# The convolution kernel's spectrum with its time signal as the stationary operand and ACT moving the result, and the first eight powers of each channel made in the setup

## The chip, the core and the metric

The kernel runs on one core of a Trainium2 chip. The metric is the device time of one execution in microseconds. A core has TensorE (PE, matrix products into PSUM; PEld are its weight loads), VectorE (DVE), ScalarE (ACT), GpSimd (POOL) and SyncE (SP, which here issues nearly all DMAs). Each has its own in-order instruction queue and they wait for each other by semaphores.

## What is computed

Two pairs of layers on 2048 tokens of 512 channels, all float32: a long convolution (an S4D layer) and then a feed-forward layer for the two tokens with the highest router score. Both pairs use the same weights. The part that matters here is the convolution and its kernel `K`:

```python
dt = jnp.exp(log_dt)
A = -jnp.exp(log_A_real) + 1j * A_imag
C = (C_real + 1j * C_imag) * dt[:, None]
P = jnp.exp((A * dt[:, None])[:, :, None] * pos[None, None, :])   # 512 channels, 128 states, 2048 positions
K = 2.0 * jnp.einsum("dn,dnl->dl", C, P).real
Kf = jnp.fft.rfft(K, L2)
Uf = jnp.fft.rfft(u_t, L2)
y = jnp.fft.irfft(Uf * Kf[None, :, :], L2)[:, :, :L]
return y + u * D_skip[None, None, :]

x = x + _A_ref(_layernorm(x), ...)
x = x + _B_ref(_layernorm(x), ...)     # two routed tokens
x = x + _A_ref(_layernorm(x), ...)
x = x + _B_ref(_layernorm(x), ...)
```

`K` doesn't depend on the tokens. The kernel makes its spectrum once, uses it in the first convolution as it comes and keeps it in DRAM (`kfd`) for the second.

## The kernel before

**Chunks and steps.** The 512 channels are four chunks of 128. The kernel's spectrum is made in 32 steps of sixteen channels (`KStep`, L434; eight steps a chunk). A position is written as `64 a + b`, with 32 values of `a` (coarse) and 64 of `b` (fine): with 128 states on the partitions, a step makes coarse and fine powers of sixteen channels (32 rows of 32 powers) and contracts them over the states to 32 x 64 values a channel.

**Setup** (`setup`, L324) computes for each channel and state a phase and a decay, and from them planes: plane 0 the start, planes 1 to 6 the steps of 1, 2, 4, ... powers (phases as shifted integers, decays as repeated products), as coarse and fine pairs. Chunk 0's planes go straight into `pi` and `pf` in SBUF (`direct`). Those of chunks 1 to 3 are made beside the first steps, in room that other tiles need later, stored in DRAM (`pid`, `prd`, one DMA for each plane, `put`, L345) and loaded half a chunk at a time (`load_params`, L294).

**One step u** has these parts:
- `phase_init` and `decay_init` (ACT, L446, L456) copy the starts into `ph` and `mg`; `phase` and `decay` (POOL, L452, L461) double what is there five times each, from 1 to 2, 4, 8, 16 and 32 powers, each time by one plane; a sixth `decay` makes `ml`.
- `trig` (ACT, L469): sine, absolute value and cosine of the 32 (and one) phases, into `sc`.
- `products` (DVE and POOL, L478): the decays into the sines and cosines. `ON_POOL` (L137) says which of them POOL takes.
- `contract` (PE, L491): 32 products of 128 rows into `pk`, four of 32 columns beside each other; ACT copies `pk` into `kt`.
- `spectrum` (L501): DVE adds the skip weight `D_skip` at position 0 of `kt`; then eight PE products with the constant `d1k` as the stationary operand (64 columns) and `kt` as the moving one (128 columns, 64 apart) into `kq`.
- `turn` (DVE, L514): a transpose in 32 by 32 blocks from `kq` into `gk`, the chunk's whole first stage.

`pk` and `kq` have one buffer each; `ph`, `mg`, `ml`, `sc` and `kt` two.

**Pipeline.** `slot(t)` (L720) issues step t-1's `spectrum`, step t's `products`, step t+1's `trig`, `phase_init` of t+3, `decay_init` of t+2, `phase` of t+2 and `decay` of t+1 in turns, then the `turn` of t-1 and the `contract` of t, with the convolution's own work between these at the places that `CONV1` (L32) gives: normalization (ACT), first stage `zf` (PE, and a DVE transpose), `kx` (the spectrum's second stage from `gk`, PE) and its way over `kfd` in DRAM back to SBUF, products with the spectrum (DVE, L568), `pv` (PE, L579), copies (ACT, L580), last stage (DVE, PE), statistics (DVE). The first six slots and the late setup are ordered by a scheduler, with `OPENING` (L112) as the order of issue; from slot 6 on DVE, ACT and POOL keep the written order (`in_order`, L211), while PE's order comes from the scheduler. When the 32 steps are done their tiles are given up, and the weights of the routed layer are loaded in their place; the rest (chunk 3's end, routed layer, second convolution, routed layer) holds no step of `KStep`.

## Time and profile before

| what | value |
| --- | --- |
| time, median of 3 runs | 697.32 us (696.2 to 698.96) |
| profiled execution, span from first to last instruction | 695.2 us |
| PE busy | 485.8 us, 70% |
| DVE busy | 580.9 us, 84% |
| ACT busy | 311.1 us, 45% |
| POOL busy | 500.4 us, 72% |
| data moved by DMA | 97.64 MB |

The profile is of one execution; its own time is its span and what lies around it, of which the page shows only the span. The runs' median is 2.1 us above that span. The page gives the span in 40 slices of 17.4 us, groups of like instructions (count, busy time, mean of one, the idle time of the engine just before them and what ended it) and DMA issues. Further views used below are busy times by stretches, the timeline of one engine, and the chain of waits that ended last.

### The profile page before, as it was taken

To read this page: it belongs to the slowest core of one execution; us is meant where nothing else is said; L and a number is where in the kernel's file an instruction comes from. 1 tells how busy PE (TensorE), PEld (TensorE's weight loads), DVE (VectorE), ACT (ScalarE), POOL (GpSimd) and SP (SyncE) were. 2 spreads that over 40 slices of the span, in tenths; PEclk is the share of its full clock that TensorE was granted. 3 is DMA by queue.
4 is the path that set the end of the run, shared out by engine and by line. 5 is a ranking of instruction groups with operands and counts; after the bars stand their busy time and mean duration, and the time that the engine had idled before them with its cause. 6 is when DMAs were issued, how large, how long until landed. Compare 5 with 4: busy or idle time off the path is not lost.

```text
span 695.2 us, 14060 instructions
## 1 busy us (share of the span) xinstructions
PE 485.8 (70%) x5300; PEld 360.2 (52%) x5300; DVE 580.9 (84%) x1164; ACT 311.1 (45%) x587; POOL 500.4 (72%) x659
## 2 busy tenths in 40 slices
PE   1012433798988898979789987267799888888336
PEld 1001322577855786648776665034678565656112
DVE  7899998687899999989999964985356799999950
ACT  4445645456753647527473121321511615214272
POOL 4879999999999999987993083260257766757252
PEclk9999775699998989979999998769599899999858
DMA  7961204768410977109460699600813748438436
GB/s 212 225 150 72 90 30 144 262 195 234 118 33 28 218 214 171 53 16 245 117 172 2 184 307 345 164 2 11 178 55 86 154 103 176 145 98 239 108 79 180
DMA packets 51709, 97.64 MB, mean 140 GB/s; under 512 B 4885, under 2 KB 35513, under 8 KB 47161
## 3 DMA queue, kind: packets, MB, share of 16 engines
q1 hardware_dynamic: 51512, 96.72, 51.5%
q8 instruction: 42, 0.69, 0.4%
q14 instruction: 27, 0.21, 0.1%
q0 software_dynamic: 128, 0.02, 0.0%
HBM read 70.23 MB, written 26.48 MB: 139 GB/s over the span
## 4 chain that ended last, share of the span: by engine, by line
DVE 33%; POOL 21%; DMA 16%; PE 14%; issue 8%; SPq 6%; ACT 1%; POOLq 0%; DVEq 0%; ACTq 0%
POOL mg L465 6%; DVE vt L638 6%; POOL ph L454 6%; PE zf L593 4%; DVE g L597 3%; DMA x<-in_x 3%; DVE jn L654 3%; DMA xw<-xs 3%; DVE p L609 3%; SPq L561 3%; DMA kf<-kfd 3%; DMA x<-xs 3%; POOL sc L482 2%; POOL ml L467 2%; DVE p L568 2%
## 5 line engine op out<-in xcount | busy, mean ns | idle before, releaser
L465 POOL TENSOR_TENSOR mg<-mg,pf 128x128 f32<-128x128 f32 (+4 forms) x160 | 108.6, 682 | 5.4 <-ACT pf L423 3.1
L454 POOL TENSOR_TENSOR ph<-ph,pi 128x512 int32<-128x512 int32 (+4 forms) x160 | 112.0, 702 | 0.5
L497 PE MATMUL pk<-sc 128*32 128x64 f32 x2048 | 46.3, 247 | 74.2 <-DVE sc L489 63.5
L618 POOL TENSOR_TENSOR y<-p 64x256 f32<-64x256 f32 x76 | 55.9, 736 | 50.0 <-DVE p L609 35.6
L507 PE MATMUL kq<-kt,d1k 128*64 128x128 f32 x512 | 63.4, 402 | 30.8 <-DVE kt L503 22.5
L593 PE MATMUL zf<-z,d 128*128 128x256 f32 x256 | 80.1, 453 | 5.9 <-DVE g L597 5.1
L497 PEld LDWEIGHTS pk<-sc 128*32 128x32 f32 x2048 | 38.4, 126 | 87.8 <-issue 57.8
L638 DVE STREAM_TRANSPOSE vt<-v 128x512 f32<-128x512 f32 x64 | 69.2, 1098 | 3.3 <-ACT v L626 2.5
L597 DVE STREAM_TRANSPOSE g<-zf 128x512 f32<-128x512 f32 x64 | 65.9, 1051 | 7.0 <-PE zf L593 7.0
L626 ACT ACTIVATE v<-pv 128x512 f32<-128x512 f32 x40 | 23.7, 596 | 97.9 <-PE pv L625 97.9
L593 PEld LDWEIGHTS zf<-z,d 128*128 128x128 f32 x256 | 52.7, 222 | 24.9 <-DVE g L597 11.7
L507 PEld LDWEIGHTS kq<-kt,d1k 128*64 128x64 f32 x512 | 40.1, 159 | 46.7 <-DVE kt L503 25.2
L640 PE MATMUL po<-vt,d 128*64 128x256 f32 x256 | 45.0, 432 | 23.1 <-DVE vt L638 22.6
L619 POOL TENSOR_TENSOR y<-p 64x256 f32<-64x256 f32 x76 | 55.6, 731 | 4.6
L625 PE MATMUL pv<-y,w 128*128 128x128 f32 x320 | 54.8, 302 | 5.0 <-POOL y L619 3.7
L524 PE MATMUL pu<-g,w 128*64 128x128 f32 x640 | 50.2, 298 | 10.2 <-DVE g L1297 3.6
L489 DVE TENSOR_TENSOR sc<-mg,sc 128x1024 f32<-128x1024 f32 x32 | 57.3, 1790 | 0.0
L625 PEld LDWEIGHTS pv<-y,w 128*128 128x128 f32 x320 | 45.1, 201 | 19.6 <-POOL y L619 9.5
L482 POOL TENSOR_TENSOR sc<-mg,sc 128x512 f32<-128x512 f32 x25 | 40.8, 1631 | 12.3 <-ACT sc L476 12.3
L609 DVE TENSOR_TENSOR p<-pu,kf 128x1024 f32<-128x1024 f32 x32 | 38.4, 1209 | 12.8 <-PE pu L524 6.2
L524 PEld LDWEIGHTS pu<-g,w 128*64 128x64 f32 x640 | 38.7, 147 | 18.4 <-DVE p L609 6.2
L579 PE MATMUL pv<-p,w 128*128 128x128 f32 x192 | 40.7, 296 | 7.5 <-DVE p L568 7.1
(344 smaller groups left out, 1175.0 us busy)
## 6 DMA issues: line engine op xcount, KB each, us to landing
kf<-kfd SPq DMA_DIRECT2D x144, 128.0 KB, 4.0
kfd<-kd SPq DMA_DIRECT2D x16, 512.0 KB, 6.8
wd<-in_wd SPq DMA_DIRECT2D x4, 1792.0 KB, 14.0
w<-in_w SPq DMA_DIRECT2D x2, 2048.0 KB, 11.1
x<-in_x SPq DMA_DIRECT2D x8, 512.0 KB
xc<-in_x SPq DMA_DIRECT2D x8, 512.0 KB, 6.0
z<-in_x SPq DMA_DIRECT2D x8, 512.0 KB, 6.4
xs<-xc SPq DMA_DIRECT2D x8, 512.0 KB, 4.3
```

Of the source, the lines that this page charges most:

```text
L454: G.tensor_tensor(self.ph[:, :, n : 2 * n], self.ph[:, :, 0:n], self.step_of(self.pis, k + 1, n), op=OP.add)
L465: G.tensor_tensor(mg[:, :, n : 2 * n], mg[:, :, 0:n], self.step_of(self.pfs, k + 1, n), op=OP.mult)
L489: V.tensor_tensor(sc[:, :, :, at], m.rearrange("p (o d) i -> p o d i", o=1).to_broadcast([128, 2, 16, 32]), sc[:, :, :, at], op=OP.mult)
L497: T.matmul(pk[32 * g : 32 * g + 32, e, :], t[:, 0:32], t[:, 33:97], start=k == 1, stop=k == 0, tile_position=(0, 32 * g))
L507: T.matmul(self.pq[64 * h : 64 * h + 64, :, 4 * g : 4 * g + 4], d1k[:, 64 * g : 64 * g + 64], kt[:, :, 32 - 32 * h : 64 - 32 * h].rearrang ...
L524: T.matmul(pt[64 * par : 64 * par + 64, ri, q, :], w2[:, k1, 64 * ri : 64 * ri + 64], src[:, k1, :], start=True, stop=True, tile_position= ...
L593: T.matmul(pf[:, 16 * s : 16 * s + 16, :], d1[:, 128 * s : 128 * s + 128], z[:, :, 16 * q : 16 * q + 16], start=True, stop=True)
L597: V.transpose(g[:, :, 16 * q : 16 * q + 16].rearrange("p k e -> p e k"), pf.rearrange("p b e -> p e b"))
L609: V.tensor_tensor(pp, pu.rearrange("p (o r) q e -> p o r (q e)", o=1).to_broadcast([128, 2, 2, 2 * CH]), kf.rearrange("p r (o q) e -> p r ...
L618: E.tensor_tensor(y[0:64, :, par, :], p1[ls, 0], p2[ls, 1], op=OP.subtract)
L625: T.matmul(pv[:, k, :], w3[:, 4 * gi + k, :], y[:, k // 2, k % 2, :], start=True, stop=True)
L638: V.transpose(vt.rearrange("p b e -> p e b"), v[:, :, es].rearrange("p k e -> p e k"))
```

## The change

1. `contract` and `spectrum`: the skip weight is added by 16 more products a step, with 4 rows and one column, into `pk` between the two halves of each accumulation (the constants are the columns of `sm` from 200 on). In `spectrum` the operands change places: `kt` is stationary (64 columns), `d1k` moves (128 columns, contiguous), and `kq` comes out with its frequencies along the free dimension. `kt` is written in the order in which it is then loaded.
2. `turn`: one ACT copy from `kq` to `gk` instead of the DVE transpose. The constants `d1`, `d1k`, `d4`, `w2` are reordered for it.
3. `setup`: eight powers (planes 0 to 7) of each channel are made on POOL (`first_eight`) for phases and decays, and three more planes (8 to 10) hold the steps of 8, 16 and 32: 11 planes instead of 7, in `pi`, `pf`, `pid` and `prd`. For chunks 1 to 3 planes 0 to 3 and 4 to 7 are stored by one DMA each.
4. A step starts with eight powers: `phase_init` and `decay_init` copy eight planes, and `phase` and `decay` double twice instead of five times. `sc` and `ph` lose the extra column.
5. The memory kept for descriptors of GpSimd's DMAs is set to 4096 bytes.

```diff
     for s in range(2):
         for h in range(2):
-            d1[s, h, :, s, h, 0, :] = np.cos(th)
-            d1[s, h, :, s, h, 1, :] = -np.sin(th)
-    d1k = np.zeros((4, 32, 4, 2, 32))
+            d1[s, h, :, s, 0, h, :] = np.cos(th)
+            d1[s, h, :, s, 1, h, :] = -np.sin(th)
+    d1k = np.zeros((4, 32, 2, 4, 32))
     for g in range(4):
-        d1k[g, :, g, 0, :] = np.cos(th)
-        d1k[g, :, g, 1, :] = -np.sin(th)
+        d1k[g, :, 0, g, :] = np.cos(th)
+        d1k[g, :, 1, g, :] = -np.sin(th)
...
-        pf = kp.tile([128, 2, 7, 64, 2], F32, name="pf", tag="pf")
-        pi = kp.tile([128, 2, 7, 64, 2], I32, name="pi", tag="pi")
+        pf = kp.tile([128, 2, 11, 64, 2], F32, name="pf", tag="pf")
+        pi = kp.tile([128, 2, 11, 64, 2], I32, name="pi", tag="pi")
...
+            def first_eight(t, dt_, steps, op, store):
+                s03, s47 = powers(t, (0, 4), 10, dt_), powers(t, (4, 8), 20, dt_)
+                flat = lambda v: v.rearrange("p e t -> p (e t)")
+                for lo, hi, w, dst in ((0, 1, 0, 1), (0, 2, 1, 2), (0, 4, 2, None)):
+                    m = hi - lo
+                    if direct:
+                        st_ = half(steps[w]).rearrange("p h (o e) t -> p h o (e t)", o=1)
+                        for h in range(2):
+                            d_ = s47[:, h] if dst is None else s03[:, h, dst : dst + m]
+                            G.tensor_tensor(d_, s03[:, h, lo:hi], st_[:, h].to_broadcast([128, m, n]), op=op)
+                    else:
+                        d_ = s47 if dst is None else s03[:, dst : dst + m]
+                        G.tensor_tensor(d_, s03[:, lo:hi], flat(steps[w]).rearrange("p (o e) -> p o e", o=1).to_broadcast([128, m, 2 * n]), op=op)
+                    if dst == 2:
+                        put(store, (0, 4), s03)
+                put(store, (4, 8), s47)
...
+            isteps = [pair(i).bitcast(I32) for i in (0, 18, 2)]
+            for k, d in enumerate(isteps):
+                V.tensor_scalar(d, ip, k + 1, None, op0=OP.logical_shift_left)
+            yield
+            V.tensor_scalar(gi, g1, -(2.0**32), None, op0=OP.mult)
+            V.tensor_tensor(bi[:, :, 0], bi[:, :, 0], gi, op=OP.add)
+            if direct:
+                V.tensor_scalar(pi[:, :, 0], half(bi), 1, None, op0=OP.logical_shift_left)
+                for k in range(3):
+                    V.tensor_scalar(pi[:, :, 8 + k], half(ip), 4 + k, None, op0=OP.logical_shift_left)
+            else:
+                V.tensor_scalar(powers(pi, (0, 4), 10, I32)[:, 0].rearrange("p (e t) -> p e t", t=2), bi, 1, None, op0=OP.logical_shift_left)
+                V.tensor_scalar(ip, ip, 4, None, op0=OP.logical_shift_left)
+                put(pid, (8, 9), ip.rearrange("p e (o t) -> p o (e t)", o=1))
+            first_eight(pi, I32, isteps, OP.add, pid)
...
+            fsteps = [pair(i) for i in (2, 0, 18)]
             for k in range(1, 7):
-                d = fplane(k)
-                A.activation(d, half(pb), AF.Identity, bias=onet)
-                put(prd, k, d)
+                d = fsteps[k - 1] if k < 4 else pf[:, :, 4 + k] if direct else pair((28, 2, 0)[k - 4])
+                A.activation(d, half(pb) if k > 3 and direct else pb, AF.Identity, bias=onet)
+                if k == 3:
+                    first_eight(pf, F32, fsteps, OP.mult, prd)
+                if k > 3 and not direct:
+                    put(prd, (4 + k, 5 + k), d.rearrange("p e (o t) -> p o (e t)", o=1))
...
             def phase_init(self):
-                self.ph = kp.tile([128, 32, 33], I32, name=f"ph{self.u}", tag="ph", bufs=KB)
+                self.ph = kp.tile([128, 32, 32], I32, name=f"ph{self.u}", tag="ph", bufs=KB)
                 A.activation(
-                    self.ph.bitcast(I16).rearrange("p d (i h) -> p d i h", h=2)[:, :, 0:33:32, :],
-                    self.pis.bitcast(I16).rearrange("p k (d h) -> p d k h", h=2)[:, :, 0:7:6, :], AF.Copy)
+                    self.ph.bitcast(I16).rearrange("p d (i h) -> p d i h", h=2)[:, :, 0:8, :],
+                    self.pis.bitcast(I16).rearrange("p k (d h) -> p d k h", h=2)[:, :, 0:8, :], AF.Copy)
 
             def phase(self, k):
-                n = 1 << k
-                G.tensor_tensor(self.ph[:, :, n : 2 * n], self.ph[:, :, 0:n], self.step_of(self.pis, k + 1, n), op=OP.add)
+                n = 8 << k
+                G.tensor_tensor(self.ph[:, :, n : 2 * n], self.ph[:, :, 0:n], self.step_of(self.pis, k + 8, n), op=OP.add)
 
             def decay_init(self):
                 self.mg = kp.tile([128, 32, 32], F32, name=f"mg{self.u}", tag="mg", bufs=KB)
                 self.ml = kp.tile([128, 16, 32], F32, name=f"ml{self.u}", tag="ml", bufs=KB)
-                A.activation(self.mg[:, :, 0], self.pfs[:, 0, :], AF.Copy)
+                A.activation(self.mg[:, :, 0:8], self.pfs[:, 0:8, :].rearrange("p k d -> p d k"), AF.Copy)
 
             def decay(self, k):
                 mg = self.mg
-                if k < 5:
-                    n = 1 << k
-                    G.tensor_tensor(mg[:, :, n : 2 * n], mg[:, :, 0:n], self.step_of(self.pfs, k + 1, n), op=OP.mult)
+                if k < 2:
+                    n = 8 << k
+                    G.tensor_tensor(mg[:, :, n : 2 * n], mg[:, :, 0:n], self.step_of(self.pfs, k + 8, n), op=OP.mult)
                 else:
-                    G.tensor_tensor(self.ml, mg[:, 1:32:2, :], self.pfs[:, 6, 1:32:2].rearrange("p (d o) -> p d o", o=1).to_broadcast([128, 16, 32]), op=OP.mult)
+                    G.tensor_tensor(self.ml, mg[:, 1:32:2, :], self.pfs[:, 10, 1:32:2].rearrange("p (d o) -> p d o", o=1).to_broadcast([128, 16, 32]), op=OP.mult)
...
             def contract(self):
                 pk = psk.tile([128, 4, 64], F32, name=f"pk{self.u}", tag="pk")
                 for e in range(4):
-                    for k in (1, 0):
+                    for k in (1, None, 0):
                         for g in range(4):
-                            t = self.sc[:, k, 4 * g + e, :]
-                            T.matmul(pk[32 * g : 32 * g + 32, e, :], t[:, 0:32], t[:, 33:97], start=k == 1, stop=k == 0, tile_position=(0, 32 * g))
-                self.kt = kp.tile([128, 4, 64], F32, name=f"kt{self.u}", tag="kt", bufs=2)
-                A.activation(self.kt, pk, AF.Copy)
+                            at, gs = pk[32 * g : 32 * g + 32, e, :], (0, 32 * g)
+                            if k is None:
+                                T.matmul(at[:, 32:33], sm[0:4, 200 + 32 * g : 232 + 32 * g], dskt[:, self.u, e : e + 1], start=False, stop=False, tile_position=gs)
+                            else:
+                                t = self.sc[:, k, 4 * g + e, :]
+                                T.matmul(at, t[:, 0:32], t[:, 32:96], start=k == 1, stop=k == 0, tile_position=gs)
+                self.kt = kp.tile([128, 4, 2, 32], F32, name=f"kt{self.u}", tag="kt", bufs=2)
+                A.activation(self.kt, pk.rearrange("p e (h b) -> p e h b", h=2)[:, :, ::-1, :], AF.Copy)
 
             def spectrum(self):
-                kt = self.kt
-                V.tensor_tensor(kt[:, :, 32], kt[:, :, 32], dskt[:, self.u, :], op=OP.add)
-                self.pq = psk.tile([128, 32, 16], F32, name=f"kq{self.u}", tag="kq")
-                for g in range(4):
-                    for h in range(2):
+
+                self.pq = psk.tile([128, 4, 4, 32], F32, name=f"kq{self.u}", tag="kq")
+                for e in range(4):
+                    for ri in range(2):
                         T.matmul(
-                            self.pq[64 * h : 64 * h + 64, :, 4 * g : 4 * g + 4],
-                            d1k[:, 64 * g : 64 * g + 64],
-                            kt[:, :, 32 - 32 * h : 64 - 32 * h].rearrange("p e b -> p b e"),
-                            start=True, stop=True, tile_position=(0, 64 * h),
+                            self.pq[64 * ri : 64 * ri + 64, e].rearrange("p g k -> p (g k)"),
+                            self.kt[:, e].rearrange("p h b -> p (h b)"),
+                            d1k[:, 128 * ri : 128 * ri + 128],
+                            start=True, stop=True, tile_position=(0, 64 * ri),
                         )
 
             def turn(self):
                 if self.s == 0:
                     gks[self.c] = new_big(f"gk{self.c}", "C")
-                V.transpose(gks[self.c][:, :, 16 * self.s : 16 * self.s + 16].rearrange("p k e -> p e k"), self.pq.rearrange("p b e -> p e b"))
+                A.activation(
+                    gks[self.c][:, :, 16 * self.s : 16 * self.s + 16].rearrange("p k (g e) -> p e g k", g=4),
+                    self.pq, AF.Copy)
...
             for k in range(5):
-                at(t + 2, "phase", k)
-                yield
-                at(t + 1, "decay", k)
-                yield
-            at(t + 1, "decay", 5)
+                if k < 2:
+                    at(t + 2, "phase", k)
+                yield
+                if k < 2:
+                    at(t + 1, "decay", k)
+                yield
+            at(t + 1, "decay", 2)
...
-    nc = bacc.Bacc("TRN2", target_bir_lowering=False, num_devices=1)
+    nc = bacc.Bacc("TRN2", target_bir_lowering=False, num_devices=1, dynamic_dma_scratch_size=4096)
```

90 lines of the change are left out of this document (43 added, 47 removed).

## The prediction

> **What bounds the kernel now.** I read the 40 slices first, then the busy time by stretches cut at four copies of `kt` (steps 8, 16, 24, 31), then the groups with shapes kept apart, then the timeline of each engine around step 6. The page:
>
> ```profile
> span 695.2 us, 14060 instructions
> ...
> PE   1012433798988898979789987267799888888336
> ...
> DVE  7899998687899999989999964985356799999950
> ...
> POOL 4879999999999999987993083260257766757252
> PEclk9999775699998989979999998769599899999858
> ```
>
> A slice is 17.4 us. POOL is at nine tenths from slice 4 to slice 18, about 50 to 310 us; DVE joins it from slice 11. That is the kernel pipeline, which ends near 383 us. The stretches (columns: length, then busy us of PE, PE's weight loads, DVE, ACT, POOL, then clock):
>
> ```profile
> 128.50:147.80 19.30, 15.39 (x200) 11.67 (x200) 15.79 (x15) 10.12 (x16) 19.14 (x25) 0.82 0.61 243
> 147.80:231.15 83.35, 73.01 (x967) 57.27 (x966) 72.66 (x86) 48.37 (x82) 82.25 (x107) 0.94 0.46 122
> 231.15:316.50 85.35, 74.51 (x962) 58.35 (x961) 81.91 (x123) 47.98 (x81) 82.64 (x105) 0.90 0.53 136
> 316.50:383.00 66.50, 58.92 (x828) 47.60 (x826) 65.41 (x98) 37.69 (x65) 48.02 (x59) 0.97 0.48 128
> 383.00:695.20 312.20, 230.11 (x1784) 157.88 (x1784) 230.85 (x618) 102.28 (x247) 156.81 (x223) 0.86 0.55 146
> ```
>
> See who is full: from 147.8 to 231 POOL alone (82.25 of 83.35); to 316.5 POOL and DVE (82.64 and 81.91 of 85.35); to 383 DVE (65.41 of 66.50). PE is third throughout: 73.01 + 74.51 + 58.92 = 206.4 of 235.2 us, 88%. So whatever leaves POOL and DVE is worth at most what PE leaves free. The 312 us behind 383 issue none of the changed steps, and there the program order of both kernels is the same; I count that part as unchanged.
>
> **The change, part by part.** Removed, per step of sixteen channels:
>
> ```profile
> L517 DVE STREAM_TRANSPOSE gk<-kq 128x512 f32<-128x512 f32 x32 | 34.5, 1079 | 2.3 <-PE kx L533 1.2 <-PE kq L507 1.1
> ...
> L454 POOL TENSOR_TENSOR ph<-ph,pi 128x32 int32<-128x32 int32 x32 | 16.9, 529 | 0.0
> L454 POOL TENSOR_TENSOR ph<-ph,pi 128x64 int32<-128x64 int32 x32 | 15.7, 491 | 0.1
> L465 POOL TENSOR_TENSOR mg<-mg,pf 128x128 f32<-128x128 f32 x32 | 15.7, 490 | 0.2
> L465 POOL TENSOR_TENSOR mg<-mg,pf 128x32 f32<-128x32 f32 x32 | 15.1, 473 | 3.6 <-ACT mg L459 1.8 <-ACT pf L423 1.8
> L454 POOL TENSOR_TENSOR ph<-ph,pi 128x128 int32<-128x128 int32 x32 | 14.9, 467 | 0.2
> ...
> L503 DVE TENSOR_TENSOR kt<-kt,dskt 128x4 f32<-128x4 f32 x32 | 14.1, 442 | 8.8 <-ACT kt L499 8.8
> ...
> L465 POOL TENSOR_TENSOR mg<-mg,pf 128x64 f32<-128x64 f32 x32 | 13.7, 429 | 1.4 <-ACT pf L423 1.4
> ```
>
> POOL loses three phase and three decay doublings, 529 + 491 + 467 + 473 + 429 + 490 = 2879 ns a step, 92 us in all. DVE loses the transpose and the skip addition, 1079 + 442 = 1521 ns a step, 48.7 us. From step 8 to step 31 (23 steps) POOL falls from 212.9 to about 147 us and DVE from 220.0 to 185. PE's 206 is then the fullest engine, so **PE is late next**.
>
> ACT gets the moved result, and wider starts:
>
> ```profile
> L540 ACT ACTIVATE kd<-kx 128x512 f32<-128x512 f32 x32 | 18.4, 594 | 33.7 <-PE kx L533 14.5 <-PE kx L524 10.8 <-DVE p L609 5.4
> ...
> L448 ACT ACTIVATE ph<-pi 128x128 int16<-128x128 int16 x32 | 9.9, 312 | 0.9
> ...
> L459 ACT ACTIVATE mg<-pf 128x32 f32<-128x32 f32 x32 | 8.1, 256 | 53.9 <-DVE sc L489 38.9 <-POOL sc L482 9.3 <-DMA pf<-prd 5.3
> ```
>
> The copy out of `kq` is 128x512 from PSUM, as L540's: 0.594 us. The phase start grows to 512 int16 (0.594 against 0.312), the decay start to 256 elements (between 0.256 and 0.594, say 0.4). Together about +1.0 us a step: ACT goes from 134 of 235 us to 157. It stays covered under PE; without cover it would cost 23 us. The new waiting instruction is the copy, which waits for `kq`; behind it on ACT stand that step's `kt` copy and copies out of `pv`, and PE waits for both. `kq` now waits for one copy less (the skip addition stood between), so I take no loss.
>
> PE exchanges the operands of `kq` and gets 16 four-row products a step:
>
> ```profile
> L507 PE MATMUL kq<-kt,d1k 128*64 128x128 f32 x512 | 63.4, 402 | 30.8 <-DVE kt L503 22.5 <-DVE gk L517 8.3
> ...
> L524 PE MATMUL pu<-g,w 128*64 128x128 f32 x640 | 50.2, 298 | 10.2 <-DVE g L1297 3.6 <-DVE g L597 3.6 <-DVE p L609 2.9
> ```
>
> ```profile
> 257.23 1.10 PE L497 MATMUL pk<-sc 128*32 128x64 f32 x64
> 258.26 0.49 PE L579 MATMUL pv<-p,w 128*128 128x128 f32 x2
> 258.59 0.39 PE L579 MATMUL pv<-p,w3b 128*128 128x128 f32 x2
> 258.81 0.39 PE L579 MATMUL pv<-p,w 128*128 128x128 f32 x2
> ...
> 260.15 1.06 PE L533 MATMUL pu<-g,w 128*128 128x128 f32 x8
> ```
>
> ```profile
> 511.57 1.15 PE L1296 MATMUL pc<-b,selT 8*128 8x128 f32 x8
> 512.65 1.13 PE L593 MATMUL zf<-z,d 128*128 128x256 f32 x4
> ```
>
> A product is two records. `kq` now moves a strided `kt` (63.4 / 256 = 0.248 us each). L524 has the shape that the new `kq` has, 64 stationary columns and 128 contiguous moving ones: 50.2 / 320 = 0.157. Eight a step save 0.73 us (bounds: 0 if the gain isn't from the stride, 0.73). The small products: 64 records of `pk` take 1.03 us to the next start, 16 ns each; 32 more records are 0.52 us even with one column instead of 64 (bounds 0 and 0.52). Then they cut `pk` into nine pieces, eight changes of shape a step. What a change costs is not shown for four rows. Upper bound: the first `pv` after `pk` takes 0.33 us to the next start, later ones 0.22, so 0.11. Lower: the patch product with 8 rows between full ones takes 1.08 us to the next start, where 8 records of full 128x128 take 1.06 with their tail, so 0.02 or less. I take 0.02, the nearest case: few rows between full products. PE a step: -0.73 + 0.52 + 0.16 = -0.05, over 23 steps 206.4 - 1.2 = 205.2 us.
>
> The Trainium skill's page "TensorEngine Tiling (Array Packing)", section "Key Properties", speaks against the small products: a change of tiling mode drains the TensorE. By that rule each of the eight changes would cost the upper 0.11 us or more; the rows for `pv` after `pk` agree with it, the patch row doesn't.
>
> How full can PE get? An engine that bounds here reaches 96 to 98% (DVE 81.91 of 85.35, 65.41 of 66.50). PE depends on more engines; I take 95%: 205.2 / 0.95 = 216 us where there were 235.2. **Steps 8 to 31: -19 us.**
>
> The setup for chunks 1 to 3 pays for the removed doublings:
>
> ```profile
> L454 POOL TENSOR_TENSOR ph<-ph,pi 128x512 int32<-128x512 int32 x32 | 41.2, 1286 | 0.1
> ...
> L465 POOL TENSOR_TENSOR mg<-mg,pf 128x512 f32<-128x512 f32 x32 | 38.5, 1205 | 0.1
> ...
> L369 POOL TENSOR_TENSOR su_w<-su_w 128x384 f32<-128x384 f32 x1 | 1.4, 1390 | 0.0
> ```
>
> It makes 768, 1536 and 3072 elements, twice: 5376 each of phases and decays. At 512 elements in 1286 and 1205 ns that is 13.5 + 12.7 = 26 us of POOL (39 at L369's rate). The first chunk's own setup adds 2 x 896 elements twice, some 9 us, ahead of step 0, where POOL has room; it makes step 0 some 5 us late. Steps 1 to 7 save 7 x 2.9 = 20 us, so POOL reaches step 6's products (L486, in the chain of waits) at about the old time:
>
> ```profile
> 121.50 1.53 POOL sc L486
> ```
>
> But in the changed program order the last three decay multiplications (12.7 us) stand behind those products: done near 121 + 12 = 133. Then come their store and the load of the first planes of chunk 1, for which ACT waits in order:
>
> ```profile
> 128.41 0.26 ACT L459 ACTIVATE mg<-pf 128x32 f32<-128x32 f32 x1 [5.30 <-DMA pf<-prd]
> 128.54 0.37 ACT L499 ACTIVATE kt<-pk 128x256 f32<-128x256 f32 x1
> ...
> 147.83 0.38 ACT L499 ACTIVATE kt<-pk 128x256 f32<-128x256 f32 x1
> ```
>
> ```profile
> w<-in_w SPq DMA_DIRECT2D x2, 2048.0 KB, 11.1
> ...
> prd<-su_w3b SPq DMA_DIRECT2D x7, 384.0 KB, 2.6
> ...
> pf<-prd SPq DMA_DIRECT2D x6, 448.0 KB, 3.7
> ```
>
> The store of four planes is one DMA of 1536 KB (between 2.6 and 11.1 us, by size 8), and SP sends the load behind it, 704 KB instead of 448, 5 us. So L459's wait ends near 133 + 13 = 146 where it ended at 128.4, and behind it on ACT stands the `kt` copy of step 6, then the `sc` of step 8: PE's `kq` and the next `pk` (one buffer) wait for those. Up to there +17. While ACT waits POOL goes through step 7's decays and products, which took most of its 19.14 us up to step 8's copy; so the two steps to 147.83 shrink from 19.3 to about 9, and step 8's copy comes near 155: **+7 us** (bounds +17, nothing caught up, and 0, if POOL's long operations run faster than its 512s).
>
> **Sum:** +7 - 19 = -12 us; span 695.2 to 683. The runs shown have the median 697.3, 2.1 us over the profiled span; with the same distance I predict **685 us**.
>
> **The rivals.**
> 1. *Changes of shape on PE cost more than the saved strides* (ends slower). For: PE is the next bound, and `pv` after `pk` shows 0.11 us. Against: the patch row. Place: `pk`, every step. It costs 8 x 0.15 = 1.2 us a step with a drain each way a little over the row: PE 206.4 + 23 x (1.2 - 0.21) = 229.2, over 0.95 = 241, +6; with the opening +13: **710 us**. At 0.11 it is 702; from about 0.085 us a change nothing is won.
> 2. *The wait at the setup isn't caught up*: +17 - 19 = -2, **695 us**. For: the same ACT queue feeds three later steps. Against: POOL's 19.14 of 19.30 us there, part of which is then already done.
> 3. *PE's clock rises as its gaps close.* The stretches show 0.94, 0.90 and 0.97 granted. If PE's busy time shrank with it: 68.6 + 67.1 + 57.2 = 192.9, less 1.2, over 0.95 = 202, so -33 + 7: **671 us**. Against: the 0.97 stretch is no denser than the others. "TensorE: Matmul & The Clock Gate" of the Trainium skill, section "What's actually happening", says that activity releases the throttle; slices 5 to 8 (clock 5 to 7 tenths, PE mostly under half busy) agree, the first four (9, PE almost idle) don't.
>
> **How the numbers follow.** Forecast 0.58 (own range 676 to 693), rival 1 0.15, rival 2 0.15, rival 3 0.12. Range 668 to 704: it takes in rivals 2 and 3 and the lower part of rival 1. Over 0.5% is 3.5 us, about what a measurement tells from no change: faster 0.56 + 0.12 = 0.68 (the forecast's upper edge touches the band), same 0.15 + 0.02 = 0.17, slower 0.15.
>
> **What would show it.** Right: POOL's busy time falls by some 60 us and DVE's by some 49; `kq` groups fall to about 1.2 us for 16 records; PE is the fullest engine from step 8 on, over 90%; a wait of ACT for the load of `pf` near 130 to 146; step 31's copy near 371; the 312 us behind it unchanged. Wrong: if the last part moves by over 3 us, if ACT's copy of `kq` takes over 1 us, if PE stays below 88% while POOL and DVE have room (then a chain of waits sets the pace and the gain is smaller), or if `pk` with its small products takes over 2.2 us a step.

## The result, and the profile after

The changed kernel takes **736.26 us** (median of 4, 735.34 to 740.6) against 697.69 us before: 1.0571 times the time, 95% interval 1.053 to 1.0611 (the quotient of the two medians alone is 1.055). It is slower by 5.7%; 685 was forecast, and 704 was the range's upper end. The profiled execution spans 733.6 us. The page of the changed kernel, its busy times and slices (18.3 us each):

```profile
span 733.6 us, 15909 instructions
...
PE 500.8 (68%) x6324; PEld 376.6 (51%) x6324; DVE 571.7 (78%) x1101; ACT 357.2 (49%) x619; POOL 454.6 (62%) x482
...
PE   1001545408999898988899896718779797978436
...
DVE  6899699975377997799796882697536699999960
...
POOL 4579799988766846876557125524054874758342
```

See the hole in PE's row: slice 9 (counted from 1, 147 to 165 us) is 0 where the row of before has a 9. It is the stretch ahead of step 6. ScalarE's timeline there (start, duration, and in brackets how long the engine stood idle before it and for what):

```profile
166.93 0.66 ACT L493 ACTIVATE mg<-pf 128x256 f32<-128x256 f32 x1 [10.80 <-DMA pf<-prd]
...
168.32 0.41 ACT L537 ACTIVATE kt<-pk 128x256 f32<-128x256 f32 x1
...
185.09 0.38 ACT L537 ACTIVATE kt<-pk 128x256 f32<-128x256 f32 x1
```

The load of the first planes of chunk 1 ends ScalarE's wait at 166.9 us (128.4 before); step 6's copy of `kt` follows at 168.3 (128.5) and step 8's at 185.1 (147.8). Step 31's comes at 418.8 (382.9). The stretches from step 8 to 31 and behind it (length, then busy us of PE, its weight loads, DVE, ACT, POOL):

```profile
185.09:418.81 233.72, 211.89 (x3486) 173.19 (x3486) 188.08 (x256) 166.00 (x247) 150.82 (x137) 0.94 0.50 135
418.81:733.60 314.79, 228.65 (x1780) 157.60 (x1780) 225.89 (x612) 103.25 (x248) 156.47 (x223) 0.86 0.55 144
```

So the time went here: **+37.3 us up to step 8's copy, -1.3 in steps 8 to 31, +2.4 behind them** (from copy to copy), together the 38.4 between the two spans. In steps 8 to 31 GpSimd and VectorE lost about what was forecast (150.8 and 188.1 us busy, forecast 147 and 185), and the pace did not change. What the changed parts cost by groups:

```profile
L535 PE MATMUL pk<-sc 128*32 128x64 f32 x2048 | 71.4, 251 | 85.0 <-DVE sc L523 80.9 <-DVE sc L520 4.0
L544 PE MATMUL kq<-d1k,kt 128*64 128x128 f32 x512 | 44.3, 328 | 9.1 <-ACT kt L537 9.1
L554 ACT ACTIVATE gk<-kq 128x512 f32<-128x512 f32 x32 | 34.1, 1065 | 4.2 <-PE kq L544 4.0
L532 PE MATMUL pk<-dskt,sm 4*32 4x1 f32 x1024 | 33.5, 182 | 0.0
```

The products of `kq` got cheaper (44.3 us in all, 63.4 before), the first stage dearer. PE's records overlap, so its two groups (71.4 and 33.5 us) can't be added up. The time in which at least one product of `pk` runs, before, in the changed kernel and in e1 below (columns: length, PE, its weight loads, ScalarE's copies):

```profile
0.00:695.20 695.20, 46.34 (x2048) 38.36 (x2048) 12.18 (x32) 0.88 0.52 140
0.00:733.60 733.60, 87.60 (x3072) 63.84 (x3072) 12.39 (x32) 0.87 0.52 142
0.00:724.40 724.40, 56.42 (x3072) 48.65 (x3072) 12.47 (x32) 0.86 0.53 144
```

So the first stage went from 46.3 to 87.6 us.

The late setup (powers of chunks 1 to 3) in the timeline, in two stretches of it:

```profile
124.49 0.98 DVE L444 TENSOR_SCALAR su_w<-su_bigB 128x768 int32<-128x768 int32 x1
...
126.35 7.11 POOL L363 TENSOR_TENSOR su_bigB<-su_w3b,su_w 128x3072 int32<-128x3072 int32 x1
126.86 7.02 DVE L444 TENSOR_SCALAR su_w3b<-su_bigB 128x768 int32<-128x768 int32 x1
...
137.33 1.33 POOL L520 TENSOR_TENSOR sc<-ml,sc 128x512 f32<-128x512 f32 x1
...
139.24 0.53 DVE L449 SCALAR_TENSOR_TENSOR su_w3b<-su_w,dtb 128x384 f32<-128x384 f32 x1
```

```profile
139.69 14.88 DVE L460 SCALAR_TENSOR_TENSOR su_w<-su_w 128x768 f32<-128x768 f32 x4
139.93 6.49 POOL L363 TENSOR_TENSOR su_w3b<-su_w3b,su_w 128x768 f32<-128x768 f32 x2 [1.27 <-DVE su_w3b L449]
...
146.49 7.26 POOL L363 TENSOR_TENSOR su_bigB<-su_w3b 128x3072 f32<-128x3072 f32 x1
...
154.67 0.94 ACT L454 ACTIVATE su_w<-su_w,cst 128x768 f32<-128x768 f32 x1 [3.61 <-DVE su_w L460]
...
156.01 0.43 SPq L349 DMA_DIRECT2D prd<-su_bigB  x1
...
162.12 1.04 SPq L297 DMA_DIRECT2D pf<-prd  x2
```

Read it as a chain: GpSimd's last phases end at 133.5, its part of step 6's products (L520) starts at 137.3 (121.5 before), the decays' start (L449) is made only at 139.2, GpSimd's decays end at 153.75, the last store is issued at 156.0, the load at 162.1, and it has landed at 166.9. Before the change the last decay step was made at 115.7 us. PE has step 6's products done at 145.9, so step 6's copy stands some 22 us behind the load only because ScalarE takes its work in the written order; no run put the copy ahead of that load's reader.

### The profile page after: what moved, and what is told of

Its sections match the earlier page's. It is cut to its first block, busy times and chain, and to the rows that moved or that the text cites. A ratio compares the mean times of both kernels' runs of the same rounds, so it can differ in the third digit from the quotient of the medians.

```text
span 733.6 us, 15909 instructions
## 1 busy us (share of the span) xinstructions
PE 500.8 (68%) x6324; PEld 376.6 (51%) x6324; DVE 571.7 (78%) x1101; ACT 357.2 (49%) x619; POOL 454.6 (62%) x482
## 4 chain that ended last, share of the span: by engine, by line
DVE 35%; PE 29%; DMA 18%; ACT 6%; issue 5%; SPq 5%; POOL 0%; POOLq 0%; DVEq 0%; ACTq 0%
PE pv L618 6%; PE zf L632 4%; DVE vt L677 4%; PE pk L535 4%; DVE g L636 3%; DMA x<-in_x 3%; DMA xw<-xs 3%; DVE sc L523 3%; DMA wgu<-in_wu 3%; PE kq L544 3%; DMA x<-xs 3%; DVE p L648 3%; DVE jn L693 2%; DVE su_w L460 2%; PE pu L563 2%
## 5 line engine op out<-in xcount | busy, mean ns | idle before, releaser
L535 PE MATMUL pk<-sc 128*32 128x64 f32 x2048 | 71.4, 251 | 85.0 <-DVE sc L523 80.9
L632 PE MATMUL zf<-z,d 128*128 128x256 f32 x256 | 77.2, 438 | 41.1 <-DVE g L636 36.2
L535 PEld LDWEIGHTS pk<-sc 128*32 128x32 f32 x2048 | 41.8, 122 | 95.9 <-issue 88.1
L632 PEld LDWEIGHTS zf<-z,d 128*128 128x128 f32 x256 | 50.1, 213 | 56.6 <-DVE g L636 40.8
L488 POOL TENSOR_TENSOR ph<-ph,pi 128x256 int32<-128x256 int32 (+1 forms) x64 | 63.1, 988 | 22.7 <-ACT ph L482 22.7
L499 POOL TENSOR_TENSOR mg<-mg,pf 128x256 f32<-128x256 f32 (+1 forms) x64 | 66.9, 1047 | 14.9 <-ACT mg L493 14.9
L679 PE MATMUL po<-vt,d 128*64 128x256 f32 x256 | 45.2, 434 | 19.3 <-DVE vt L677 19.1
L523 DVE TENSOR_TENSOR sc<-mg,sc 128x1024 f32<-128x1024 f32 x32 | 56.4, 1762 | 2.1 <-ACT sc L510 2.1
L607 DVE TENSOR_TENSOR p<-pu,kf 128x1024 f32<-128x1024 f32 x24 | 28.9, 1217 | 34.4 <-PE pu L572 15.8
L544 PE MATMUL kq<-d1k,kt 128*64 128x128 f32 x512 | 44.3, 328 | 9.1 <-ACT kt L537 9.1
L648 DVE TENSOR_TENSOR p<-pu,kf 128x1024 f32<-128x1024 f32 x32 | 38.5, 1212 | 12.5 <-PE pu L563 5.5
L501 POOL TENSOR_TENSOR ml<-mg,pf 128x512 f32<-128x512 f32 x32 | 46.4, 1450 | 2.0
```

Source lines behind the costliest of these rows:

```text
L488: G.tensor_tensor(self.ph[:, :, n : 2 * n], self.ph[:, :, 0:n], self.step_of(self.pis, k + 8, n), op=OP.add)
L499: G.tensor_tensor(mg[:, :, n : 2 * n], mg[:, :, 0:n], self.step_of(self.pfs, k + 8, n), op=OP.mult)
L523: V.tensor_tensor(sc[:, :, :, at], m.rearrange("p (o d) i -> p o d i", o=1).to_broadcast([128, 2, 16, 32]), sc[:, :, :, at], op=OP.mult)
L535: T.matmul(at, t[:, 0:32], t[:, 32:96], start=k == 1, stop=k == 0, tile_position=gs)
L544: T.matmul(self.pq[64 * ri : 64 * ri + 64, e].rearrange("p g k -> p (g k)"), self.kt[:, e].rearrange("p h b -> p (h b)"), d1k[:, 128 * ri ...
L632: T.matmul(pf[:, 16 * s : 16 * s + 16, :], d1[:, 128 * s : 128 * s + 128], z[:, :, 16 * q : 16 * q + 16], start=True, stop=True)
```

## The experiments

Two theories, which can both hold. **L**: the late setup's chain ends in the load for which ScalarE stands in order before step 6's copy, and that is the +37 us. **S**: TensorE pays for each change between 128-row and 4-row products, eight a step, and that eats what steps 8 to 31 had won. The rivals are named in the runs: the opening (chunk 0's own powers) delays everything (O), the small products themselves cost (P), or ScalarE's dearer copy does (A).

All runs in one table; copies are the starts of ScalarE's `kt` copy, from the profiled execution of each. A ratio is to the runs of the kernel before that were made beside that run (their medians lie from 697.1 to 699.6 us), so it isn't a quotient of the times in the table.

| run | time, us | ratio to before (95%) | step 0 | step 6 | step 8 | 8 to 31 |
| --- | --- | --- | --- | --- | --- | --- |
| before | 697.7 | | 51.7 | 128.5 | 147.8 | 235.1 |
| changed | 736.3 | 1.0571 (1.053 to 1.0611) | 80.9 | 168.3 | 185.1 | 233.7 |
| e1 128-row products | 726.0 | 1.0399 (1.0351 to 1.0447) | 81.3 | 169.5 | 186.6 | 222.2 |
| e2 no small products | 722.7 | 1.0349 (1.0308 to 1.0389) | 61.6 | 163.1 | 182.5 | 223.6 |
| e3 setup alone | 727.5 | 1.0402 (1.0359 to 1.0446) | 63.4 | 167.4 | 187.1 | 227.8 |
| e4 spectrum alone | 707.8 | 1.0105 (1.0078 to 1.0133) | 55.9 | 129.7 | 149.5 | 244.7 |
| e5 chunk 0 singly | 721.6 | 1.0333 (1.0286 to 1.038) | 58.4 | 163.9 | 179.0 | 225.6 |
| e6 chunks 1-3 singly | 712.0 | 1.0212 (1.0174 to 1.0249) | 83.4 | 140.7 | 161.0 | 237.1 |
| e7 = e4, 128-row | 703.7 | 1.0091 (1.0058 to 1.0124) | 55.5 | 129.2 | 150.8 | 237.0 |
| e8 powers at load, GpSimd | 715.5 | 1.0261 (1.0226 to 1.0296) | 58.8 | 132.7 | 157.1 | 232.8 |
| e9 no late phases | 714.6, one run | | 80.8 | 157.2 | 172.2 | 227.3 |
| e10 late powers on VectorE | 720.2 | 1.0318 (1.0262 to 1.0373) | 81.4 | 160.7 | 178.0 | 229.4 |
| e11 = e7, copy order | 701.4 | 1.0059 (1.0021 to 1.0096) | 56.4 | 130.0 | 148.9 | 232.9 |
| e12 = e8 on VectorE | 723.4 | 1.0376 (1.0328 to 1.0424) | 58.0 | 132.0 | 151.9 | 255.1 |
| e13 no late decays | 727.7, one run | | 81.7 | 166.7 | 182.3 | 228.6 |
| e14 no late powers | 709.9, one run | | 81.5 | 151.4 | 168.4 | 225.5 |
| e15 four powers | 715.3 | 1.0221 (1.0181 to 1.026) | 59.2 | 148.4 | 165.2 | 235.4 |
| e16 exchange and copy only | 691.9 | 0.9881 (0.985 to 0.9913) | 52.5 | 129.6 | 148.3 | 227.1 |

### The four parts (e1 to e4)

e1, on the changed kernel:

```diff
-        dskt = kp.tile([4, 32, 4], F32, name="dskt", tag="dskt")
+        dskt = kp.tile([128, 32, 4], F32, name="dskt", tag="dskt")
-        nc.sync.dma_start(dskt.rearrange("p s e -> p (s e)"), dsk)
+        G.memset(dskt, 0.0)
+        nc.sync.dma_start(dskt[0:4].rearrange("p s e -> p (s e)"), dsk)
-  T.matmul(at[:, 32:33], sm[0:4, 200 + 32 * g : 232 + 32 * g], dskt[:, self.u, e : e + 1], ...)
+  T.matmul(at[:, 32:33], sm[:, 200 + 32 * g : 232 + 32 * g], dskt[:, self.u, e : e + 1], ...)
```

> The changed kernel, but the skip weight's small products read all 128 rows (weights in rows 0 to 3, zeros below), so their count stays at 16 a step and the shape of TensorE's tile never changes within a step. Theory S (the change of tile shape from 128 to 4 rows and back, 8 times a step, is what TensorE pays): first stage with small products falls from the 104.9 us of the changed kernel to about 60 us (46.3 as before the change, plus 512 small products at about 0.03 us), steps 8 to 31 from 233.7 to 205-215 us, time 708-720 us; step 8's copy stays near 180. Rival P (the small products themselves, or ScalarE's dearer copy, set the pace, whatever their rows): first stage stays above 95 us, steps 8 to 31 stay at 230-236 us, time 732-740 us.

e2, on the changed kernel: `for k in (1, 0)` in `contract`, and in `spectrum`

```diff
+  V.tensor_tensor(self.kt[:, :, 0, 0], self.kt[:, :, 0, 0], dskt[:, self.u, :], op=OP.add)
```

> The changed kernel without small products: VectorE adds the skip weight to the kernel tile after ScalarE's copy, as in the kernel before. Theory S and the rival that the products cost by themselves both expect the first stage at about 46 us of TensorE, steps 8 to 31 at 203-215 us, time 705-720 us; set beside the run with 128-row products it prices the products alone (equal within 5 us under S, 20 us or more apart under the rival). Rival A (ScalarE's copy of the spectrum, 1.07 us a step in its queue, sets the pace): steps 8 to 31 stay at 230-236 us, time 732-742 us.

e3 is the kernel before with items 3 to 5 of the change, e4 with items 1 and 2.

> The kernel before with only the powers made once in the setup and the shorter doublings (first stage of the spectrum, its turn on VectorE and the skip add as before). Theory O (the setup's new chain delays steps 0 and 6): step 0's copy near 80 and step 8's near 180 us, both some 30 us behind the kernel before; steps 8 to 31 at 212-222 us, since VectorE and GpSimd do less and TensorE has no small products; time 705-722 us. Rival (the delay comes from the spectrum's part, which makes the first steps longer on TensorE): step 8's copy at 148-160 us, time 678-695 us.

> The kernel before with only the spectrum's first stage changed (kernel stationary, 16 small products of 4 rows a step, ScalarE's copy). Theory S and O together: step 8's copy at 148-156 us, and steps 8 to 31 at 235-250 us, since TensorE's 206.4 us of busy time grow by about 28 us (1.83 more a step in the first stage, 0.6 less in the spectrum) and meet GpSimd's unchanged work; time 697-715 us. Rival (the spectrum's part causes the late opening): step 8's copy at 170 us or later, time 725 us or more.

Of e1, the groups of the first stage and the stretch from step 8 to 31:

```profile
L535 PE MATMUL pk<-sc 128*32 128x64 f32 x2048 | 55.7, 245 | 90.0 <-DVE sc L523 85.3 <-DVE sc L520 4.5 <-issue 0.2
...
L532 PE MATMUL pk<-dskt,sm 128*32 128x1 f32 x1024 | 34.5, 178 | 0.0
```

```profile
186.57:408.81 222.24, 191.95 (x3484) 162.20 (x3482) 184.85 (x254) 165.91 (x248) 151.45 (x137) 0.95 0.52 142
```

The count of products is the same; only their rows differ. PE's busy time in steps 8 to 31 falls from 211.9 to 192.0 us, (211.9 - 192.0) / (23 x 8) = 0.108 us a change, and the stretch from 233.7 to 222.2. That the change of shape costs, and not the four-row products themselves, shows in PE's timeline, the changed kernel first, then e1:

```profile
271.79 0.43 PE L535 MATMUL pk<-sc 128*32 128x64 f32 x16
272.15 0.24 PE L532 MATMUL pk<-dskt,sm 4*32 4x1 f32 x8
272.32 0.43 PE L535 MATMUL pk<-sc 128*32 128x64 f32 x16
```

```profile
269.96 0.41 PE L535 MATMUL pk<-sc 128*32 128x64 f32 x16
270.18 0.22 PE L532 MATMUL pk<-dskt,sm 128*32 128x1 f32 x8
270.24 0.41 PE L535 MATMUL pk<-sc 128*32 128x64 f32 x16
```

Sixteen records of 128 rows take 0.36 us to the next start beside 4-row ones and 0.22 in e1, though they are the same products; eight small ones take 0.17 and 0.06. Both sides of a change pay.

S holds in the pace, though 222.2 us is more than the 205 to 215 expected. The time falls by 10 us to 726 (the ratios don't overlap), not to 720: step 8 stays at 186.6. The first stage falls from 87.6 to 56.4 us, near the 60 expected. Taking the products out as well (e2, 722.7 us, also over its range) changes the pace by 1.4 us, and its interval overlaps e1's, so P falls here. And A falls as the whole cause: both runs leave the copy as it is and win.

The setup alone and the spectrum alone, steps 8 to 31:

```profile
187.10:414.89 227.79, 207.71 (x2748) 164.26 (x2746) 203.96 (x301) 145.40 (x224) 144.55 (x134) 0.91 0.53 141
```

```profile
149.52:394.19 244.67, 215.13 (x3488) 178.77 (x3488) 185.42 (x257) 153.13 (x246) 203.33 (x267) 0.93 0.45 121
```

The setup alone has the whole delay (step 8 at 187.1) and wins 7.3 us afterwards, though GpSimd works 68 us less; the spectrum alone has no delay and loses 9.6 us afterwards. PE's busy time there grows by 9 us (215.1, 206.4 before) and not by the 28 expected, which came from adding up overlapping records. By the medians the parts add up: +29 and +9 against +39. e3's time, 727.5, is over its range: its steps win less than the 13 to 23 us that I had expected. Its step 0 comes at 63.4 and not near 80, and step 8 is as late all the same, a first sign against O. In e2, too, step 0 comes at 61.6. Both make chunk 0's powers in the setup, but have no small products; so 18 to 19 of the 29 us at step 0 come only with both parts together, in the order that the scheduler then gives the opening (in the changed kernel step 0's products end at 74.5 us and its copy starts at 80.9, behind other work of ScalarE). No run takes that apart.

### Which setup (e5 to e7)

e5 and e6 stand on e1. Channels marked `one` start from one power and double five times as before:

```diff
+                self.one = self.c == 0          # e6: self.c > 0
+                self.n8 = 1 if self.one else 8
...
+                if self.one:
+                    n = 1 << k
+                    G.tensor_tensor(self.ph[:, :, n : 2 * n], self.ph[:, :, 0:n], self.step_of(self.pis, (1, 2, 3, 8, 9)[k], n), op=OP.add)
```

(the same for decays), and `setup` makes no first eight for them (e6 stores and loads planes 0 to 3 and 8 to 10, and makes them in room that no pending store holds). e7 is e4 with e1's edit, so neither.

> The kernel with 128-row products, with chunk 0's powers doubled one by one again (eight short doublings a step back, no first eight in the opening's setup); chunks 1 to 3 keep their stored powers. Theory L (the late setup's chain, ending with the load for which ScalarE waits before step 6's copy, is what costs, and the opening's delay is swallowed by that wait): step 0's copy at 52-66 us instead of 81.3, step 6's still at 160-170, time 716-727 us. Rival O (the opening's delay is carried through): step 6's copy at 138-146, time 698-706 us.

> The kernel with 128-row products, with chunks 1 to 3 doubled one by one again (seven planes stored and loaded, no first eight in the late setup); chunk 0 keeps its powers made in the opening's setup. Theory L: step 0's copy near 81 us as in the changed kernel, but step 6's at 132-148, so that most of the 38 us go; steps 8 to 31 at 228-237 us, since GpSimd has its doublings back; time 700-714 us. Rival O: step 6's copy at 158 or later, time 722 us or more.

> The kernel before with only the spectrum's first stage changed, as in the run of the spectrum alone, but with 128-row small products. Theory S (tile-shape changes are the spectrum part's cost): steps 8 to 31 fall from 244.7 to 230-236 us, step 8's copy at 146-151, time 692-700 us. Rival A (ScalarE's strided copy, 1.07 us, costs as much): steps 8 to 31 stay at 240-246, time 703-710 us.

ScalarE's timeline, e5 first, then e6:

```profile
162.53 0.64 ACT L513 ACTIVATE mg<-pf 128x256 f32<-128x256 f32 x1 [16.20 <-DMA pf<-prd]
163.90 0.41 ACT L560 ACTIVATE kt<-pk 128x256 f32<-128x256 f32 x1
```

```profile
140.66 0.38 ACT L561 ACTIVATE kt<-pk 128x256 f32<-128x256 f32 x1 [0.16 <-PE pk L559]
```

Step 6's copy in the four cases: neither 129.2, chunk 0 alone 140.7, late chunks alone 163.9, both 169.5. So **the late chunks bring 29 to 35 us and chunk 0 brings 6 to 12** (169.5 - 163.9 and 140.7 - 129.2); with chunk 0's part gone the wait for the load only grows (16.2 instead of 11.7 us) and most of the start's gain is swallowed. L holds against O. In the medians e6's 14 us are less than the 29 at step 6, since with the doublings back steps 8 to 31 take 237.1 us. e7's steps 8 to 31 fall from 244.7 to 237.0 in the profiles, but its time overlaps e4's, so with GpSimd full the shape changes are not shown to cost time. Its steps lie between what S and A expected, its time in A's range.

### What stands in the late chain (e9, e10, e13, e14)

All stand on e1. e9 leaves out `first_eight`'s late operations for the phases, e13 for the decays, e14 both; e10 puts them on VectorE:

```diff
-                        G.tensor_tensor(d_, s03[:, lo:hi], flat(steps[w])..., op=op)
+                        if op == OP.mult:       # e9; e13: op == OP.add; e14: never
+                            G.tensor_tensor(d_, s03[:, lo:hi], flat(steps[w])..., op=op)
+                        V.tensor_tensor(d_, s03[:, lo:hi], flat(steps[w])..., op=op)   # e10 instead
```

> The kernel with 128-row products, leaving out the three operations on GpSimd that make the first eight phases of chunks 1 to 3 (their planes are stored as eight copies of the first, so the stores keep their size and the phases of steps 8 to 31 are wrong). Theory L, in its strong form: the phases' 13.8 us on GpSimd (115.38 to 133.46 us in the changed kernel) and the 7.02 us for which a VectorE operation lasts beside them stand ahead of the decays' start, so that start moves from 139.2 to 120-130 us and step 6's copy from 169.5 to 149-160; time 706-717 us. Rival D (only the decays' own powers, their stores and the load are on the chain): step 6's copy at 163 or later, time 720-728 us.

> The kernel with 128-row products, leaving out the three late operations on GpSimd that make the first eight decays of chunks 1 to 3 (stores of the same size, from the first plane; the decays of steps 8 to 31 are wrong). Theory L (all late powers stand one behind the other): the 13.75 us from 139.93 to 153.75 go, but the decay steps on ACT and VectorE then end the chain near 147, so step 6's copy falls from 169.5 to 155-162 us, time 710-720 us. Rival (the phases' part alone makes the wait): step 6's copy at 166 or later, time 722 us or more.

> The kernel with 128-row products, leaving out all six late operations on GpSimd (phases and decays of steps 8 to 31 are wrong; stores and loads keep their size). Theory L: what is left is chunk 0's delay (the run with late chunks doubled singly has step 6's copy at 140.7 us) and the larger stores and loads, so step 6's copy at 140-150 us, time 696-710 us. Rival (stores, loads and their order are the main part): step 6's copy at 153 or later, time 712 us or more.

> The kernel with 128-row products, with the late setup's first eight (phases and decays of chunks 1 to 3) on VectorE instead of GpSimd. Theory L with GpSimd's rate and its hold on VectorE as the cause: 3072 elements take some 3.3 us instead of 7.1 to 7.3, the decay steps on VectorE last about 1 us again (not 3 to 5), step 6's copy falls from 169.5 to 143-156 us, time 701-715 us. Rival (the extra work is on the chain on whichever engine, and VectorE is the fuller one there): step 6's copy at 160 or later, time 718 us or more.

The end of ScalarE's wait in e9, e13 and e14:

```profile
155.84 0.64 ACT L494 ACTIVATE mg<-pf 128x256 f32<-128x256 f32 x1 [17.17 <-DMA pf<-prd]
```

```profile
165.37 0.63 ACT L494 ACTIVATE mg<-pf 128x256 f32<-128x256 f32 x1 [8.11 <-DMA pf<-prd]
```

```profile
150.01 0.63 ACT L494 ACTIVATE mg<-pf 128x256 f32<-128x256 f32 x1 [11.95 <-DMA pf<-prd]
```

Against e1's 169.5 for step 6, leaving out the phases' powers is worth 12.3 us, the decays' 2.8, both 18.1. In e9 the decays' start is made at 127.9 us, 11.7 us earlier than in e1 (139.6), and step 6 follows. e13 missed its range (155 to 162), and its numbers are its rival's: the decays start only at 139.97, as in e1, since the phases' powers stand ahead of them. The 2.8 us is not the whole weight of the decays' own operations, though. Without them the last plane is made at 146.8 us, 9.1 us earlier than in e1, but SP issues its store only at 154.8 and the load at 160.4 (163.4 in e1); why it does so late stays open. With no late power at all step 6 comes at 151.4, a little over the range, and 10.7 us behind e6, which stores and loads seven planes. That rest goes with the eleven planes' stores and loads and their order; I have not split it further.

e10 missed too, and its numbers are its rival's (the extra work is on the chain on whichever engine). In its timeline (VectorE's last power, the last store, the load):

```profile
140.85 3.34 DVE L363 TENSOR_TENSOR su_bigB<-su_w3b 128x3072 f32<-128x3072 f32 x1
...
146.48 0.33 SPq L349 DMA_DIRECT2D prd<-su_w  x1
...
154.54 1.04 SPq L297 DMA_DIRECT2D pf<-prd  x2
```

3072 elements take 3.34 us instead of 7.26, and the decay steps last 0.9 to 2 us again, but step 6 is only 8.8 us earlier: the load is issued 8 us behind the last store. GpSimd's rate can be part of L, not the whole.

### Other ways to have the powers (e8, e12, e15)

e8 makes eight powers in place from seven loaded planes, for 64 channels at a time, from step 12 on; e12 does so on VectorE; e15 makes four late powers instead of eight, keeps chunk 0 single and has the copy of e11 below.

```diff
+        def eight(t, op, h):
+            p = t[:, h].rearrange("p k e t -> p k (e t)")
+            for lo, hi, w, d in ((0, 1, 1, 1), (0, 1, 3, 2), (1, 2, 3, 3), (0, 3, 7, 4), (3, 4, 7, 7)):
+                m = hi - lo
+                G.tensor_tensor(p[:, d : d + m], p[:, lo:hi], p[:, w : w + 1].to_broadcast([128, m, 128]), op=op)
```

> 128-row small products; chunk 0 and the first half of chunk 1 doubled one by one, and from step 12 on the first eight powers made on GpSimd in place for 64 channels, in the steps after each load (about 2.1 us for the phases and 2.1 us for the decays once in four steps, worked out from 2.3 ns an element in the changed kernel's 3072-element operation), with nothing more in the setup or in the stored planes. If both theories hold (L and S): step 8's copy at 146-155, steps 8 to 31 at 220-230 us, time 682-694 us. Rival (the steps' pace gains nothing when GpSimd does less): steps 8 to 31 at 233 us or more, time 695 us or more.

> The run with the powers made in place after each load, with those ten operations on VectorE instead of GpSimd, where 128 elements took 0.80 us each. Theory: GpSimd's 195 us of work in steps 8 to 31 fall to about 152, VectorE's grow from 195 by about 12; step 8's copy comes at 147-153 instead of 157.1 us, steps 8 to 31 take 222-229 instead of 232.8 us, time 688-704 us. Rival (VectorE sets the pace): steps 8 to 31 at 233 or more, time 710 us or more.

> The spectrum changed, with 128-row products and the copy in runs of four; chunk 0 doubled one by one; for chunks 1 to 3 four powers instead of eight (2304 elements of phases and of decays on GpSimd instead of 5376, eight planes instead of eleven), so a step loses the two shortest phase and the two shortest decay doublings. Theory L: step 6's copy at 138-150 us instead of 163.9 with eight, steps 8 to 31 at 218-228 us, time 692-706 us. Rival (any late powers in this chain cost more than they give back): step 6's copy later than 152, time 708 us or more.

None beat the kernel before, and e8 and e12 missed what the theory expected. Of e8:

```profile
L305 POOL TENSOR_TENSOR pf<-pf 128x128 f32<-128x128 f32 x20 | 15.8, 798 | 0.8
```

```profile
157.13:389.95 232.82, 193.16 (x3492) 163.43 (x3492) 195.40 (x257) 165.73 (x246) 195.32 (x194) 0.95 0.50 130
```

A 128-element operation lasts 0.80 us in the mean (0.45 at the least), not the 0.29 that I scaled from the 3072 ones, so GpSimd is back at 195 us. On VectorE (e12) GpSimd falls to 161 us and the stretch grows to 255 us; why it grows by so much stays open. e15's wait is short as expected (step 6 at 148.4) but its steps win nothing (235.4 us); VectorE waits 26.6 us there for loads of the spectrum, 9.2 in e5. Whether its two more loads a half chunk on SP's queue do that was not tried.

### The spectrum by itself (e11, e16)

e11 is e7 with ScalarE's copy in another order; e16 has that copy, and no small products (VectorE adds the skip weight). With `g` outside `e`, as written, the expectation's runs of four follow each other, so sixteen neighbours are written in a row.

```diff
-  gks[self.c][...].rearrange("p k (g e) -> p e g k", g=4), self.pq, AF.Copy
+  gks[self.c][...].rearrange("p k (g e) -> p k g e", g=4), self.pq.rearrange("p e g k -> p k g e"), AF.Copy
```

> The kernel before with the spectrum changed and 128-row products, with ScalarE's copy written in runs of four neighbours (k, g, e) instead of element by element 512 bytes apart (e, g, k). Theory A (the copy's 1.06 us in ScalarE's queue is what eats the rest of the spectrum's gain): the copy takes 0.55-0.75 us, steps 8 to 31 fall from 237.0 to 230-234 us, time 696-701 us. Rival (ScalarE is not what the steps wait for): the copy gets shorter or not, steps 8 to 31 stay at 235-239, time 702-706 us.

> The kernel before with only the operands of the spectrum's products exchanged and the copy moved to ScalarE in runs of four; the skip weight added by VectorE as before, no small products. If the exchange and the move are a gain of their own: steps 8 to 31 at 224-232 us, time 688-696 us. Rival (GpSimd, at nine tenths there, sets the pace whatever TensorE and VectorE save): steps 8 to 31 at 233-237 us, time 696-702 us.

e11's copy, then steps 8 to 31 of e11 and of e16:

```profile
L520 ACT ACTIVATE gk<-kq 128x512 f32<-128x512 f32 x32 | 18.6, 582 | 4.1 <-PE kq L510 4.1
```

```profile
148.88:381.81 232.93, 194.92 (x3488) 167.40 (x3488) 194.15 (x257) 143.27 (x247) 213.65 (x269) 0.92 0.48 128
```

```profile
148.30:375.43 227.13, 189.04 (x2752) 158.93 (x2752) 196.08 (x279) 144.63 (x247) 219.83 (x270) 0.92 0.52 133
```

The order alone takes the copy from 1.063 to 0.582 us and the stretch from 237.0 to 232.9; by the medians e11 overlaps e7, so that 4 us is a reading of the two profiles. e16 is the version that **beats both kernels: 691.9 us, 0.9881 (0.985 to 0.9913)** of before. The exchange of operands and the move to ScalarE, in this order of the copy, are a gain of 1.2%, small but clear of the noise; the two were not run apart. GpSimd is the fullest engine again (219.8 of 227.1 us). Between e11 and e16 lie the small products and the addition that takes their place on VectorE: 5.8 us in steps 8 to 31, and ratios that don't overlap. So P, which fell beside the shorter doublings (e1 against e2), holds beside the longer ones; why it depends on that isn't settled.

## Why the prediction was wrong

- **"Step 8's copy comes near 155: +7 us" is the step that failed most; it is +37.3.** GpSimd's work was sized well (26 us forecast, 27.5 in the groups of L363), and from its last decay to the landed load took 13.2 us where I had 13. What failed is *"POOL reaches step 6's products (L486, in the chain of waits) at about the old time"*, and with it *"done near 121 + 12 = 133"*. That the decays' multiplications come behind those products was right, but the products come at 137.3 us and not 121.5, and the multiplications run from 139.9 to 153.75. Ahead of them stand the phases' powers (to 133.5, with the VectorE operation that lasts 7.02 us beside them) and a late opening: the decays' start, at 139.6 in e1, comes at 127.9 without the phases' powers (e9) and at 130.5 with chunk 0 done singly (e5). Leaving the phases' powers out moves step 6 by 12.3 us, the decays' by 2.8 (e13), doing all late chunks singly by 28.9 (e6).
- *"The two steps to 147.83 shrink from 19.3 to about 9"* failed too: from step 6's copy to step 8's it is 16.8 us. Nearly all of the wait stayed, as in rival 2, whose +17 was too small for the same reason.
- *"It makes step 0 some 5 us late"*: 29 us in the changed kernel, 10 and 12 in e2 and e3, which make the same powers without small products. Doing chunk 0 singly takes 6 to 12 us off step 6 (e1 against e5, e6 against e7).
- **"Steps 8 to 31: -19 us" gave -1.3.** PE was late next, as forecast: 211.9 of 233.7 us, 91%. The mis-sized term is *"I take 0.02"* for a change of shape: 0.108 us of PE time (e1), near the upper bound of 0.11 from `pv` after `pk`, so rival 1's mechanism. The Trainium skill's page "TensorEngine Tiling (Array Packing)", section "Key Properties", has a change of tiling mode drain the TensorE; the 0.108 us agrees with that, if 4 and 128 rows are two such modes, which the trace doesn't tell. I had taken the patch row as the nearest case and it was the wrong one. PE's other two terms came out better than forecast: without small products PE's busy time is 187.4 us (e2), so the exchange saves (206.4 - 187.4) / 23 = 0.83 us a step (0.73 forecast), and the products without a change of shape cost (192.0 - 187.4) / 23 = 0.20 (0.52 forecast). Rival 1's own formula gives 206.4 + 23 x (8 x 0.108 - 0.21) = 221.4 us busy, over 0.95 = 233, and 233.7 was measured; that is luck, since PE was busy for 211.9 us and 91% full.
- *"I take 95%"* failed as well: without the changes of shape PE is 86% busy (e1, 192.0 of 222.2) and no engine is above it, so waits between engines must set the pace; which ones, no run shows. The stretch won 12.9 us (e1) and 11.5 us (e2), not 19.
- *"0.594 us"* for ScalarE's copy: 1.065 as written, 0.582 in e11's order.
- Right: what POOL and DVE lose in steps 8 to 31; `kq` at 44.3 / 32 = 1.38 us a step (about 1.2 forecast); the last part within 3 us (+2.4); no gain from the clock (0.94 granted, about 0.93 before). Two of its signs of being wrong came true, a copy of `kq` over 1 us and `pk` at 87.6 / 32 = 2.74 us a step, and a third, PE below 88%, once the changes of shape are gone (e1).
- The totals fell by less than forecast: POOL's by 46 us and not 60, DVE's by 9 and not 49. Up to step 8's copy VectorE is busy for 157.8 us (130.1 before), and some 17 of these 28 us are operations of L444 and L460 that lengthened beside GpSimd's long ones.
- Two readings of the rows of before were loose, without weight in the sum: PE is second and not third in the first and the last of the three stretches, and slice 18 of POOL's row is an 8.

## What to carry to other kernels

When work moves from a steady loop into a setup, follow the setup's longest chain through every engine, its room and its store and load to the first in-order wait for it; the sum of one engine's time is no estimate of when that ends. Few-row products between full ones were not free on TensorE here: try giving them the rows of their neighbours (with zeros in the added rows PE's time for `pk` fell from 87.6 to 56.4 us) or leaving them to another engine. And test the parts of a change apart: here the one that paid, the exchange with the copy in another order, was hidden under two that cost.
